# Moving a streaming kernel's SBUF arena from 32 bytes past a 256-byte boundary onto the boundary

## The chip, the cores and the metric

The kernel runs on one core of a Trainium2 chip. Times are device microseconds from repeated executions. A time that I call "the span" is that of the one execution that was profiled.

## The reference, cut to what matters

The input is 384 x 384 pixels of 384 channels in bf16, 113.25 MB. The kernel takes the mean of every channel, multiplies it by one weight, passes it through a sigmoid, and multiplies every pixel by the result:

```python
g = jnp.einsum("bhwc->bc", x) / (H * W)
s = sigmoid(g * w1d[0])          # k is 1, so the padding does nothing
return x * s[:, None, None, :]
```

Each byte has to be read and each has to be written: 226.5 MB in all.

## The kernel before: the parts that matter

SBUF holds one big tensor, the arena, which is cut into six slots of 44 rows. A chunk of 128 x 44 pixels is loaded into a slot, summed by matmuls with ones, multiplied in place by an early estimate of the gate, and stored. (The gate of the whole image is compared at the end; if it differs in bf16, a second pass repairs the output. It is not needed with these inputs.) So every pixel is read once and written once.

```python
total = nc.alloc_sbuf_tensor("total", [P, C], F32)
n_arena = nc.sbuf_bytes_remaining // (2 * C)
arena = nc.alloc_sbuf_tensor("arena", [P, n_arena * C], BF16)
...
EDGE, SLOT, BOTH = 44, 44, 4
def dram(view, r0, n):       # partition p gets n rows that lie together in memory
    return view[r0 * P : (r0 + n) * P, :].rearrange("(p t) c -> p (t c)", p=P)
def at(r0, n):
    return arena[:, r0 * C : (r0 + n) * C]
...
for k in range(BOTH):        # the first four chunks: half on each queue
    load(places[k], sizes[k], starts[k], ("sync", "scalar"))
...
for k in range(1, len(sizes)):
    if k >= n_slots:
        j = k - n_slots
        put(places[j], sizes[j], starts[j], places[j])    # gate on DVE, then store on the scalar queue
    if k >= BOTH:
        load(places[k], sizes[k], starts[k])              # on the sync queue, waits for that store
    add_rows(places[k], sizes[k], 1, k == 1, k == last)   # matmuls
```

In a partition the small tensors end at byte 20,000 = 78 x 256 + 32, and the arena starts there. One DMA moves 33,792 bytes (132 x 256) in each of 128 partitions, and one such piece is one data packet in the trace. The four opening chunks go in pieces of 16,896 bytes; the last two chunks have pieces of 21,504 and 18,432 bytes. All of these are multiples of 256.

Of the kernel before, what the change touches and what calls it, by code (L numbers as in the profile page):

```python
# [3 lines left out]
P = 128  # L4
ROW = 384
BF16 = mybir.dt.bfloat16
# [108 lines left out]
def bass_standalone__channel_attn_eca__vision_kernel(  # L115
# [5 lines left out]
    B, H, W, C = x.shape  # L121
# [13 lines left out]
    wrong = nc.alloc_sbuf_tensor("wrong", [P, 1], F32)  # L135
    redo = nc.alloc_sbuf_tensor("redo", [P, 1], I32)
    total = nc.alloc_sbuf_tensor("total", [P, C], F32)
    n_arena = nc.sbuf_bytes_remaining // (2 * C)
    arena = nc.alloc_sbuf_tensor("arena", [P, n_arena * C], BF16)
    acc = [  # L140
        [nc.alloc_psum_tensor(f"acc{g}_{i}", [P, WIDE], F32) for i in range(3)]
        for g in range(2)
# [258 lines left out]
```

## Time and profile before

| | before |
|---|---|
| time, median of 3 runs | 531.62 us (531.5 to 532.85) |
| packets of the two data queues, share of 16 engines | 53.4% + 46.0% |
| PE / DVE busy | 47% / 46% |
| rate, 85 to 185 us | 432 GB/s |
| data packet of 33,792 bytes, load or store | 1251 ns in 5,671 of 5,888 |

From the page of the kernel before: the span and the engines' busy times, then the span in 40 slices of 13 us (busy tenths of the DMA engines, and what they moved), then the two data queues (packets, MB, share of the 16 engines' span; q10 is fed by ScalarE's sequencer, q1 by SyncE's).

```profile
span 529.9 us, 1954 instructions
PE 246.9 (47%) x865; PEld 96.4 (18%) x865; DVE 241.2 (46%) x45; ACT 2.7 (1%) x4; POOL 0.3 (0%) x5
...
DMA  8999999999999999999999999999999999999997
GB/s 357 430 427 412 446 429 431 446 412 444 434 426 446 413 443 444 416 444 431 429 445 416 441 439 421 446 414 441 444 416 446 427 431 444 424 429 431 444 416 331
...
q10 hardware_dynamic: 4466, 121.90, 53.4%
q1 hardware_dynamic: 3888, 104.60, 46.0%
```

The DMA engines are full in all slices but the first and the last, while PE and DVE sit idle half of the time. The list of waits of the load queue says the same from the other side; its columns are what waited, for what, how long in total, how often, and the longest.

```profile
SPq L99 <- DMA out_dram<-arena: 454.2, 21, 63.1
```

Loads wait for stores to leave their slot. The kernel is bound by the DMA engines, which spend 53.4% + 46.0% = 99.4% of the span in packets of the two data queues. So I took it that anything that shortens a packet in the steady state shortens the kernel.

### The profile page before, as it was taken

To read this page: it belongs to the slowest core of one execution; us is meant where nothing else is said; L and a number is where in the kernel's file an instruction comes from. 1 tells how busy PE (TensorE), PEld (TensorE's weight loads), DVE (VectorE), ACT (ScalarE), POOL (GpSimd) and SP (SyncE) were. 2 spreads that over 40 slices of the span, in tenths; PEclk is the share of its full clock that TensorE was granted. 3 is DMA by queue.
4 is the path that set the end of the run, shared out by engine and by line. 5 is a ranking of instruction groups with operands and counts; after the bars stand their busy time and mean duration, and the time that the engine had idled before them with its cause. 6 is when DMAs were issued, how large, how long until landed. Compare 5 with 4: busy or idle time off the path is not lost.

```text
span 529.9 us, 1954 instructions
## 1 busy us (share of the span) xinstructions
PE 246.9 (47%) x865; PEld 96.4 (18%) x865; DVE 241.2 (46%) x45; ACT 2.7 (1%) x4; POOL 0.3 (0%) x5
## 2 busy tenths in 40 slices
PE   0977174264274274364264274373263373374400
PEld 0333021121021121121021121121121121121100
DVE  0199824633624624623624615615614615617620
ACT  1000000000000000000000000000000000000000
POOL 0000000000000000000000000000000000000000
PEclk9988675786786875786786875776886876777665
DMA  8999999999999999999999999999999999999997
GB/s 357 430 427 412 446 429 431 446 412 444 434 426 446 413 443 444 416 444 431 429 445 416 441 439 421 446 414 441 444 416 446 427 431 444 424 429 431 444 416 331
DMA packets 8363, 226.62 MB, mean 428 GB/s; under 512 B 930, under 2 KB 930, under 8 KB 930
## 3 DMA queue, kind: packets, MB, share of 16 engines
q10 hardware_dynamic: 4466, 121.90, 53.4%
q1 hardware_dynamic: 3888, 104.60, 46.0%
q8 instruction: 6, 0.10, 0.1%
q14 instruction: 3, 0.02, 0.0%
HBM read 113.25 MB, written 113.25 MB: 427 GB/s over the span
## 4 chain that ended last, share of the span: by engine, by line
another core or an unknown queue 70%; DMA 16%; DVE 4%; PE 3%; issue 1%; SPq 1%; ACT 0%; ACTq 0%
DMA out_dram<-arena 8%; DMA arena<-in_x_dram 6%; PE acc L186 3%; DMA w_one<-in_w1d_dram 2%; DVE arena L156 2%; SPq L91 1%; DVE total L208 1%; ACT s_true L290 0%; ACT s_early L266 0%; DVE total L298 0%; DVE total L206 0%; DVE wrong L306 0%; ACTq L91 0%; SPq L99 0%
## 5 line engine op out<-in xcount | busy, mean ns | idle before, releaser
L186 PE MATMUL acc<-arena,ones 128*128 128x512 bf16 x864 | 246.8, 457 | 242.3 <-DMA arena<-in_x_dram 242.3
L156 DVE TENSOR_TENSOR arena<-arena,s_early 128x16896 bf16<-128x16896 bf16 (+2 forms) x27 | 234.5, 8691 | 240.3 <-PE acc L186 236.1
L186 PEld LDWEIGHTS acc<-arena,ones 128*128 128x128 bf16 x864 | 96.3, 114 | 392.3 <-DMA arena<-in_x_dram 254.5
L234 PE MATMUL w_all<-w_one,ones 1*128 1x1 bf16 x1 | 0.2, 158 | 14.4 <-DMA w_one<-in_w1d_dram 14.4
L243 DVE TENSOR_SCALAR w_scaled<-w_all 128x1 f32<-128x1 f32 x2 | 0.2, 153 | 13.6 <-PE w_all L234 13.6
L208 DVE TENSOR_TENSOR total<-total,acc 128x128 f32<-128x128 f32 (+2 forms) x11 | 4.5, 408 | 1.7 <-PE acc L186 1.4
L206 DVE COPY total<-acc 128x384 f32<-128x384 f32 x1 | 0.6, 556 | 10.0 <-PE acc L186 10.0
L290 ACT ACTIVATE s_true<-total,w_scaled 128x384 bf16<-128x384 f32 x1 | 0.6, 614 | 478.2 <-DVE total L208 478.2
L234 PEld LDWEIGHTS w_all<-w_one,ones 1*128 1x128 bf16 x1 | 0.1, 98 | 14.4 <-issue 14.4
L228 ACT ACT_TABLE_LOAD x1 | 1.3, 1283 | 3.4 <-issue 3.4
L298 DVE TENSOR_TENSOR total<-s_true,s_early 128x384 f32<-128x384 uint16 x1 | 0.6, 557 | 0.7 <-ACT s_true L290 0.7
L266 ACT ACTIVATE s_early<-total,w_scaled 128x384 bf16<-128x384 f32 x1 | 0.6, 614 | 22.7 <-DVE total L208 22.7
L306 DVE TENSOR_REDUCE wrong<-total 128x1 f32<-128x384 f32 x1 | 0.6, 553 | 0.0
L256 DVE MEMSET ones<- 128x128 bf16 x1 | 0.2, 165 | 0.8 <-PEq L386 0.8
L228 ACT ACTIVATE warm<-warm 128x1 f32<-128x1 f32 x1 | 0.2, 203 | 0.0
L312 DVE CAST redo<-wrong 128x1 int32<-128x1 f32 x1 | 0.2, 153 | 0.0
L386 POOL MEMSET const-bfloat16-1.0<- 128x1 bf16 x1 | 0.1, 102 | 0.0
L386 POOL MEMSET const-uint8-127<- 128x1 uint8 x1 | 0.1, 102 | 0.0
L386 POOL MEMSET const-float32-0.0<- 128x1 f32 x1 | 0.1, 99 | 0.2 <-issue 0.2
L386 POOL MEMSET const-float32-1.0<- 128x1 f32 x1 | 0.1, 99 | 0.0
L255 POOL MEMSET warm<- 128x1 f32 x1 | 0.1, 98 | 0.3 <-POOLq L386 0.3
## 6 DMA issues: line engine op xcount, KB each, us to landing
out_dram<-arena ACTq DMA_DIRECT2D x25, 4224.0 KB, 61.5
arena<-in_x_dram SPq DMA_DIRECT2D x21, 4224.0 KB, 39.2
arena<-in_x_dram ACTq DMA_DIRECT2D x4, 2112.0 KB, 27.5
arena<-in_x_dram SPq DMA_DIRECT2D x4, 2112.0 KB, 27.5
arena<-in_x_dram SPq DMA_DIRECT2D x1, 2688.0 KB, 35.6
out_dram<-arena ACTq DMA_DIRECT2D x1, 2688.0 KB, 30.0
arena<-in_x_dram SPq DMA_DIRECT2D x1, 2304.0 KB
out_dram<-arena ACTq DMA_DIRECT2D x1, 2304.0 KB, 27.1
```

The costliest lines, as they stand in the source:

```text
L91: ("op", lambda e: e.dma_start(out, in_), self.pool[i], 16)
L156: return lambda e: e.tensor_tensor(to_v, v, s_b, ALU.mult)
L186: lambda e, i=i, bank=bank: e.matmul(bank[:, :], ones[:], arena[:, start + i * WIDE : start + (i + 1) * WIDE], start=first and i < 3, stop ...
L206: emit = lambda e, part=part, of=of: e.tensor_copy(part, of)
L208: emit = lambda e, part=part, of=of: e.tensor_tensor(part, part, of, ALU.add)
L228: lambda e: e.activation(warm[:, 1:2], warm[:, 0:1], ACT_F.Sigmoid),
L234: lambda e: e.matmul(w_all[:, 0:1], ones[0:1, :], w_one[0:1, 0:1], start=True, stop=True),
L266: lambda e: e.activation(s_early[:], total[:], ACT_F.Sigmoid, scale=w_scaled[:, 0:1]),
L290: lambda e: e.activation(s_true[:], total[:], ACT_F.Sigmoid, scale=w_scaled[:, 1:2]),
L298: lambda e: e.tensor_tensor(total[:], s_true[:].bitcast(U16), s_early[:].bitcast(U16), ALU.not_equal),
L306: lambda e: e.reduce_max(wrong[:], total[:], axis=mybir.AxisListType.X),
L386: nc = _bacc.Bacc("TRN2", target_bir_lowering=False, num_devices=1)
```

## The change

The change puts the arena at byte 20,224 = 79 x 256. As every piece is a multiple of 256 bytes long, every transfer then has its SBUF address at a multiple of 256, where it was 32 bytes past one. (Below, "misaligned" means off a multiple of 256.) There is still room for 272 rows, so there are six slots as before, and each engine has the same instructions in the same order.

```diff
-    n_arena = nc.sbuf_bytes_remaining // (2 * C)
-    arena = nc.alloc_sbuf_tensor("arena", [P, n_arena * C], BF16)
+    n_arena = (nc.sbuf_bytes_remaining - 256) // (2 * C)
+    arena = nc.alloc_sbuf_tensor("arena", [P, n_arena * C], BF16, align_bytes=256)
```

## The prediction

> **What bounds the kernel now.** The DMA engines. The page's slices show a mean DMA busy share of 90% or more in 38 of 40 slices; PE is busy 47% of the span, DVE 46%. The queue list puts 53.4% + 46.0% = 99.4% of the 16 engines' span into packets of the two data queues. In steady state (the stretch view, 85 to 185 us) the DMA share is 1.00 at 432 to 433 GB/s; only the start (401 GB/s) and the last 8 us (352 GB/s) are lower. So the time is the sum of packet durations per DMA engine plus about 3 us.
>
> **What a packet costs.** From the trace's packet records: a row piece of 33,792 bytes takes 1251 ns in loads and stores alike (5,671 of 5,888 exactly), 21,504 bytes take 799 and 18,432 take 686. The slope is 15,360 bytes in 565 ns = 27.2 bytes per ns[...]. The intercept is 1251 - 33,792/27.2 = about 8.6 ns per packet. A 4-byte semaphore packet, which does not touch the arena, takes 9 ns, so nearly all of those 8.6 ns look like a fixed cost.
>
> **What the change does.** The arena has room for 272 rows before; 256 bytes less still leaves 272, and six slots of 44 rows. Schedule, sizes, queues and waits stay; nothing is added or removed. Every row address moves from 32 bytes past a multiple of 256 to a multiple of 256. Row pieces are multiples of 256 bytes (33,792 = 132 x 256), so today every data packet is misaligned on the SBUF side, and afterwards none is; the HBM side steps in the same multiples already. I expect the gate (8691 ns) and the matmul (457 ns) unchanged.
>
> **What it should save.** [...] An engine moves 226.5 MB / 16 / 33,792 = 419 such packets[...]; the whole intercept would be 3.6 us (0.7%). All of it lies on the critical path, because the engines are saturated. [...]
>
> **Predicted time.** 531.0 us, 0.6 below the 531.62; range 529.4 to 532.5. Faster by over 2%: 0.01; within 2%: 0.97; slower by over 2%: 0.02.
>
> **What would show it.** The 33,792-byte packet drops from 1251 to 1247-1250 ns, most likely 1250; if it does not move, misalignment costs nothing at this size. DMA share stays 99%, steady rate 433 to 434 GB/s. The numbers of packets and instructions and the load queue's wait for stores (21 waits, 454 us) stay.
>
> **What would make it wrong.** [...] If aligned rows of all partitions collide in SBUF, with each other or with DVE and PE reads, packets would grow: slower. If alignment changes the DVE's or PE's rate, it would hardly show: half their time is idle.

The forecast's sum came to a gain of 0.6 us (531.62 - 531.0), which is 1.4 ns for each of the 419 packets of an engine. Terms of that sum are cut at the marks: the saving per packet that was held most likely, and a larger one, rested on a mechanism that no run of this case shows. Of the terms only the largest still stands, the whole intercept of 8.6 ns for each packet, 3.6 us. The reason given for 2% being out of reach is cut too, because it took 27.2 bytes per ns for a limit, and the packet records show it only as the slope between two sizes.

## The result, and the profile after

| | before | after |
|---|---|---|
| median of 5 runs | 531.68 us | 531.89 us |
| range | 531.5 to 532.85 | 531.64 to 532.48 |
| ratio, 95% interval | | 1.0003 (0.9991 to 1.0015) |
| data packet of 33,792 bytes | 1251 ns in 5,671 of 5,888 | 1251 ns in 5,653 of 5,888 |
| data packet of 16,896 bytes, between 4 and 41 us | 629 ns in 447 of 935; 487 slower, mean 634.6 ns | 629 ns in 933 of 941 |

In the counts of 16,896-byte packets, here and below, the one or two of each run that took over 645 ns (653 and 1127 ns in the kernel before) are left out.

The same lines of the page after:

```profile
span 530.1 us, 1954 instructions
PE 246.3 (46%) x865; PEld 96.0 (18%) x865; DVE 241.2 (45%) x45; ACT 2.7 (1%) x4; POOL 0.3 (0%) x5
...
DMA  8999999999999999999999999999999999999997
GB/s 357 432 431 408 439 418 449 426 430 441 418 446 428 428 447 421 436 439 421 444 425 433 444 421 439 436 419 449 426 431 441 419 444 431 428 428 438 438 420 334
...
q10 hardware_dynamic: 4466, 121.90, 53.5%
q1 hardware_dynamic: 3888, 104.60, 46.0%
```

and of its load queue's waits:

```profile
SPq L99 <- DMA out_dram<-arena: 454.1, 21, 63.1
```

Nothing that bounds the kernel moved: the queues' shares, the rate and the wait are those of before. (Single slices swing between 408 and 449. My estimate from the packet size: one packet of 33,792 bytes more or less on each of 16 engines in a slice of 13.25 us is 41 GB/s. The stretch from 85 to 185 us has 432 GB/s before and 433 after, and the packet records of 100 to 450 us give 432.9 for both.) One thing did move, in the packet records: in the opening, while only loads run, half of the 16,896-byte packets of the kernel before take about 5 ns more than 629 ns, and none but a few do after. The excess adds up to 0.17 us per DMA engine, too little to see in the time.

So there are two questions. Is misalignment really free for these packets, or is it paid somewhere that does not show? And is the slow opening due to alignment, or chance?

### The profile page after: what moved, and what is told of

The parts are those of the page before. It is cut to its first block, busy times and chain, and to the rows that moved or that the text cites. A ratio compares the mean times of both kernels' runs of the same rounds, so it can differ in the third digit from the quotient of the medians.

```text
span 530.1 us, 1954 instructions
## 1 busy us (share of the span) xinstructions
PE 246.3 (46%) x865; PEld 96.0 (18%) x865; DVE 241.2 (45%) x45; ACT 2.7 (1%) x4; POOL 0.3 (0%) x5
## 4 chain that ended last, share of the span: by engine, by line
another core or an unknown queue 70%; DMA 16%; DVE 4%; PE 3%; SPq 1%; issue 1%; ACT 0%; ACTq 0%
DMA out_dram<-arena 8%; DMA arena<-in_x_dram 6%; PE acc L186 3%; DVE arena L156 3%; DMA w_one<-in_w1d_dram 2%; SPq L91 1%; DVE total L208 1%; ACT s_true L290 0%; ACT s_early L266 0%; DVE total L298 0%; DVE total L206 0%; DVE wrong L306 0%; ACTq L91 0%; SPq L99 0%
## 5 line engine op out<-in xcount | busy, mean ns | idle before, releaser
L156 DVE TENSOR_TENSOR arena<-arena,s_early 128x16896 bf16<-128x16896 bf16 (+2 forms) x27 | 234.5, 8691 | 241.2 <-PE acc L186 237.8
```

Source lines behind the costliest of these rows:

```text
L156: return lambda e: e.tensor_tensor(to_v, v, s_b, ALU.mult)
```

## The experiments

In all but the two repeats the arena is allocated at a multiple of 256 bytes with 192 bytes of room, and shifted by a constant. All outputs were correct.

### Other offsets, and the two kernels once more

```diff
-    arena = nc.alloc_sbuf_tensor("arena", [P, n_arena * C], BF16, align_bytes=256)
+    SH = 2      # e_off4: 2 elements, 4 bytes; e_off128: SH = 64
+    arena = nc.alloc_sbuf_tensor("arena", [P, n_arena * C + 96], BF16, align_bytes=256)
...
-        return arena[:, r0 * C : (r0 + n) * C]
+        return arena[:, SH + r0 * C : SH + (r0 + n) * C]
...
-        start = place * C
+        start = SH + place * C
```

In the expectations below, a descriptor is the transfer of one contiguous run, which is one packet in these traces (e_768_off0 has 295,851 packets; 226.5 MB in runs of 768 bytes are 294,912). The theories were there to be tested. A: the start address costs nothing. B: an offset of 4 bytes costs something, 32 and 128 bytes do not. C: a small cost per transfer, larger at 128 bytes past than at 32. D: a larger cost per transfer than C. The mechanisms that the theories were drawn from are cut at the marks, because no run of this case shows them; the bands that are left are my guesses.

Expected of e_off4:

> The aligned kernel with the arena shifted to 4 bytes past a multiple of 256[...]. Theory A (start address free[...]): the 33,792-byte packet stays 1251 ns, time within 0.3% of before. Theory B[...]: packet 1252 to 1260 ns, time 0.1 to 0.8% up (532 to 536 us).

Expected of e_off128:

> Arena at 128 bytes past a multiple of 256. Theories A and B: packet 1251 ns, time within 0.3% of before. Theory C[...] packet 1256 ns and time about 2 us up against the aligned kernel.

Expected of the kernel before, run again unchanged:

> The kernel before once more, for its packet records. In its first trace the 16,896-byte load packets between 22 and 42 us took 633 or 640 ns (466 of them), in the trace after all 629. If alignment does that (a cost in the load-only opening), they show 633 and 640 here again. If it was chance of that one execution, they may all show 629.

Expected of the changed kernel, run again unchanged:

> The changed kernel once more. If alignment decides the 629 against 633 or 640 ns of the load-only opening: all 629 again. If chance decides: 633 and 640 may turn up here too. 33,792-byte packets 1251 ns.

| arena, bytes past a multiple of 256 | time (ratio to before, interval) | 33,792-byte packets at 1251 ns | 16,896-byte packets from 4 to 41 us: slower than 629 ns, their mean | excess per engine | first slow ones at about |
|---|---|---|---|---|---|
| 0 (e_after_again) | one run | 5,666 of 5,888 | 4 of 941 | 0.00 us | none |
| 4 (e_off4) | 531.84 us (1.0003, 0.9989 to 1.0017) | 5,479 | 582 of 936, 635.6 ns | 0.24 us | 18 us |
| 32 (e_before_again) | one run | 5,650 | 490 of 940, 634.6 ns | 0.17 us | 21 us |
| 128 (e_off128) | 531.96 us (1.0003, 0.9989 to 1.0016) | 5,655 | 286 of 940, 634.1 ns | 0.09 us | 26 us |

The time and the whole-row packet do not depend on the offset, from 0 to 128 bytes (531.68 to 531.96 us in the four kernels timed; at 4 bytes 137 whole-row packets read 1252 ns and 25 read 1249, but the mean of all is 1252.9 ns, against 1253.0 to 1253.4 in the other five traces). The DVE gate takes 8691 ns when aligned and 8693 ns at 4 bytes past. The slow opening is alignment and not chance: both traces of the misaligned kernel have it, both of the aligned kernel lack it, and the other two offsets have it in their own size. It does not grow with the distance from the multiple of 256 below: 128 bytes past cost no more than 32. The excess is even smaller there: from 30 to 41 us, where the packets have turned slow, all of them together average 635.7, 634.6 and 632.8 ns at 4, 32 and 128 bytes, that is 6.7, 5.6 and 3.8 ns above 629 (at 128 bytes a quarter of them still take 629). Why the offset matters so is open. In the opening of every misaligned kernel here the packets, once the start is over, are at 629 ns for 15 to 24 us first; I come back to that.

### The same bytes in short runs

To make a cost per transfer visible, the next kernels move the same bytes in runs of 256 or 768 bytes (the matching reshapes of the SBUF side are left out of the diff).

```diff
 # e_768_*: row t*128+p in partition p, so that a run in memory is one row
-        return view[r0 * P : (r0 + n) * P, :].rearrange("(p t) c -> p (t c)", p=P)
+        return view[r0 * P : (r0 + n) * P, :].rearrange("(t p) c -> p t c", p=P)
 # e_256_*: three DMAs for each old one, one for each third of every row
+        v = view[r0 * P : (r0 + n) * P, :].rearrange("(p t) c -> p t c", p=P)
+        return [v[:, :, b * D : (b + 1) * D] for b in range(3)]      # D = C // 3
 # SH = 0 in e_*_off0, SH = 16 elements (32 bytes) in e_*_off32
```

Expected of e_256_off0:

> The same work moved in runs of 256 bytes (three DMAs for each old one, one per third of a row), arena at a multiple of 256. [...]if a fixed 8.6 ns comes on each as it does on a whole row, 9.4 + 8.6 = 18 ns instead of 9.4, and the time nearly doubles (about 1000 us); [...]it is between 535 and 900 us. This is the base for e_256_off32, whichever it is.

(The band of 535 to 900 us was for a fixed part that not every run pays.)

Expected of e_256_off32:

> As e_256_off0 with the arena 32 bytes past a multiple of 256: every run of 256 bytes now crosses a boundary[...]. Theory A (alignment to 256 is free): same time as e_256_off0 within 1%. Theory C[...] 6 to 12% slower than e_256_off0. Theory D[...]: over 12% slower.

Expected of e_768_off0:

> The same work moved in runs of 768 bytes (row t*128+p in partition p), arena at a multiple of 256. [...]540 to 700 us. Base for e_768_off32.

(The band came from 768 / 27.2 = 28.2 ns for the bytes of a run, and up to 8.6 ns more.)

Expected of e_768_off32:

> As e_768_off0 with the arena 32 bytes past a multiple of 256[...]. Theory A: same as e_768_off0 within 1%. Theory C: [...]3 to 4% slower. Theory D: over 4% slower.

| run | aligned | 32 bytes past | difference of the medians |
|---|---|---|---|
| 256 bytes | 792.01 us (1.4899 of before) | 836.17 us (1.5723) | 44.2 us, 5.6% |
| 768 bytes | 614.36 us (1.1562) | 625.69 us (1.1764) | 11.3 us, 1.8% |

So misalignment is not free. But neither difference is one that I had written down: 5.6% is just below the band of theory C (6 to 12%), and 1.8% lies between theory A (within 1%) and theory C (3 to 4%). The slices say why. First e_768_off0, then e_768_off32, the rate in 40 slices of the span:

```profile
GB/s 306 373 372 373 373 373 373 373 372 373 373 373 373 373 372 373 373 373 373 373 372 373 373 373 373 373 372 373 373 373 373 372 373 373 373 373 372 373 373 332
```

```profile
GB/s 277 326 326 341 373 373 373 373 372 373 373 373 373 373 372 373 373 373 373 373 372 373 373 373 373 373 372 373 373 373 372 372 373 373 373 373 372 359 324 293
```

The loss is all in the first four slices and the last three. In between, the misaligned kernel runs at exactly the rate of the aligned one. Stretches of e_768_off32 give the three parts; the columns are the stretch, its length, busy time of PE, PEld, DVE, ACT and POOL with the number of instructions, the granted TensorE clock, the DMA share and GB/s:

```profile
6.00:56.00 50.00, 29.91 (x100) 11.49 (x100) 20.89 (x11) 2.10 (x3) 0.00 (x0) 0.86 1.10 326
60.00:570.00 510.00, 212.58 (x746) 82.80 (x744) 206.51 (x24) 0.00 (x0) 0.00 (x0) 0.70 1.09 373
590.00:615.00 25.00, 0.00 (x0) 0.00 (x0) 1.26 (x3) 0.61 (x1) 0.00 (x0) 0.50 1.02 322
```

In the packet records the slow part starts at about 4.5 us and ends at 57 us, and the first store packet starts at 57.1 us. The last load packet starts at 570.3 us, and the end turns slow at about 585 us. So the cost is paid where the engines move in one direction only, and not where loads and stores alternate. The two slow parts account for the difference: 52 us x (1 - 326/373) = 6.6 us, and 37 us x (1 - 322/373) = 5.1 us, together 11.6 us before rounding, for 11.3 us measured.

The runs of 256 bytes show the same, but for small losses in the middle. The slices of e_256_off0, then of e_256_off32:

```profile
GB/s 254 289 289 278 290 290 290 290 290 290 290 290 290 289 290 290 290 290 290 289 290 290 290 290 289 290 290 290 290 290 289 290 290 290 290 289 285 289 290 238
```

```profile
GB/s 198 218 218 218 256 288 289 289 289 280 286 290 290 290 282 285 289 290 289 290 282 286 286 289 286 281 287 290 290 289 283 286 290 289 289 287 234 216 216 184
```

Three stretches of e_256_off32, loads alone, both, stores alone:

```profile
6.00:60.00 54.00, 18.77 (x67) 7.41 (x67) 2.75 (x8) 0.00 (x0) 0.00 (x0) 0.91 1.39 218
200.00:300.00 100.00, 36.06 (x127) 14.12 (x128) 26.87 (x3) 0.00 (x0) 0.00 (x0) 0.65 1.28 289
760.00:820.00 60.00, 0.00 (x0) 0.00 (x0) 0.00 (x0) 0.00 (x0) 0.00 (x0) 0.51 0.85 216
```

and those of e_256_off0:

```profile
6.00:60.00 54.00, 28.08 (x100) 11.00 (x100) 3.80 (x9) 2.10 (x3) 0.00 (x0) 0.91 1.28 289
200.00:300.00 100.00, 31.72 (x109) 12.22 (x110) 26.87 (x3) 0.00 (x0) 0.00 (x0) 0.64 1.28 290
740.00:780.00 40.00, 0.00 (x0) 0.00 (x0) 0.00 (x0) 0.00 (x0) 0.00 (x0) 0.50 1.28 290
```

In the middle, from 100 to 740 us, e_256_off32 averages 287.1 GB/s by its packet records, for 289.5 in the middle of e_256_off0, which is about 5 of the 44 us. In two of its dips, at 180 to 190 and 300 to 310 us, the load queue has 54% and 55% of the packets instead of half: there the mixture is uneven.

From the rates, the cost of one misaligned run follows (16 engines, so one engine's time per run is 16 x bytes / rate):

| run | aligned, ns per run | loads alone, 32 bytes past | extra | stores alone, extra |
|---|---|---|---|---|
| 256 bytes | 16 x 256 / 290 = 14.1 | 16 x 256 / 218 = 18.8 | 4.7 ns | 16 x 256 / 216 - 14.1 = 4.8 ns |
| 768 bytes | 16 x 768 / 373 = 32.94 | 16 x 768 / 326 = 37.69 | 4.7 ns | 16 x 768 / 322 - 32.94 = 5.2 ns |

The extra is the same for both sizes, so it is a cost per run and not per byte. (The durations of single packets are no good for this: a 256-byte packet is recorded as 18 ns while one ends every 14.1 ns. The records overlap: 18 / 14.1 = 1.28, the DMA share that the stretches of e_256_off0 show.)

### Loads and stores kept apart

That the mixture of directions hides the cost was still only read off from where the slow parts lay. A rival says that it belongs to the opening and the end of the program for some other reason, for example because the opening loads on both queues. The last four kernels load six chunks, then store all six, then load the next six, on one queue for each direction after the opening. The rival then expects nothing new in the later batches.

```diff
-    for k in range(1, len(sizes)):
-        ... (a store of chunk k-6, then the load of chunk k)
+    for b in range(0, len(sizes), n_slots):
+        ks = range(b, min(b + n_slots, len(sizes)))
+        if b:
+            for token in stored_of[-1]:      # loads wait for all stores of the last batch
+                plan._wait("sync", token)
+        ... load and add all ks (new lists of tokens)
+        for token in landed[-1]:             # stores wait for all loads of this batch
+            plan._wait("scalar", token)
+        for k in ks:
+            put(places[k], sizes[k], starts[k], places[k])
```

Expected of e_768_split_off0:

> 768-byte runs, aligned arena, but loads and stores kept apart: six chunks are loaded, then all six are stored, then the next six are loaded, in five batches. Both theories: 768-byte packets 36 ns throughout, 373 GB/s within a load or store phase, 640 to 720 us in all because of the gaps between phases. Base for e_768_split_off32.

Expected of e_768_split_off32:

> The same 32 bytes off. In e_768_off32 only the opening (326 for 373 GB/s, 4.7 ns per descriptor) and the end were slower than in e_768_off0; the stretch in which loads and stores alternate was not. Theory M (a misaligned SBUF side costs about 4.7 ns per descriptor, and shows only where an engine moves in one direction): every phase is slow, 18,432 descriptors per engine times 4.7 ns = 87 us above e_768_split_off0 (60 to 95). Theory E (it belongs to the opening and the end of a program, whatever the direction): 11 us above, as between e_768_off32 and e_768_off0.

Expected of e_row_split_off0:

> Whole rows of 33,792 bytes, aligned, loads and stores kept apart in five batches: 560 to 620 us. Packets 1251 ns in all phases. Base for e_row_split_off32.

Expected of e_row_split_off32:

> The same 32 bytes off. Theory M: in later load phases too the packets turn from 1251 to about 1255 to 1262 ns, after some 30 packets per engine if the slack of about 150 ns seen in the opening is used up again in each phase; time 0.5 to 2 us above e_row_split_off0. Theory E: 1251 ns in all phases after the opening, same time.

| loads and stores apart | aligned | 32 bytes past | difference of the medians |
|---|---|---|---|
| 768-byte runs | 642.77 us (1.2079 of before) | 728.40 us (1.3699) | 85.6 us, 13.3% |
| whole rows, 33,792 bytes | 558.59 us (1.0501) | 561.15 us (1.0550) | 2.6 us, 0.46% |

The rival expected 11 us for the first pair, the theory of the direction 87 us. 85.6 us were measured; over the 18,432 runs that each engine moves that is 4.6 ns for one. The rates in 40 slices, first of e_768_split_off0, then of e_768_split_off32:

```profile
GB/s 310 373 372 373 307 373 373 373 373 313 372 373 373 303 373 373 373 373 314 373 372 373 306 373 373 373 373 314 372 373 372 306 373 373 373 373 311 327 248 343
```

```profile
GB/s 281 326 327 326 272 325 323 325 325 287 326 326 326 268 324 323 325 325 287 326 326 326 270 324 323 324 325 285 326 326 327 272 325 325 323 325 286 326 243 305
```

The dips in both are the changes of direction. Between them every phase, loads and stores, is at 373 GB/s when aligned and at 323 to 327 when not. Nothing else differs between the two kernels, and the mixed kernels of the same run length do not show it in their middle. This settles the direction against the rival. Nor is it two queues taking turns that hides the cost: in the opening of e_768_off32, from 10 to 46 us, each queue has half of the packets (7,651 and 7,647), all of them loads, and the rate is 326 GB/s.

With whole rows the effect is as small as it should be: an engine moves 419 of them, and 419 x 4.7 ns = 2.0 us; 2.6 us were measured, and the intervals of the two ratios to before (1.0483 to 1.0518 and 1.0532 to 1.0567) do not meet. (Two expectations were narrowly missed here: 2.6 us is above the 0.5 to 2 us, and the aligned kernel's 558.59 us is below 560.) Each of the four full store phases, 48 packets per engine, is 0.23 to 0.26 us longer than in the aligned kernel, 5 ns for a packet. Its packet records show it directly:

| packets of 33,792 bytes | aligned | 32 bytes past |
|---|---|---|
| second load phase, 150 to 165 us | all 192 at 1251 ns | 173 of 192 at 1251 ns |
| second load phase, 165 to 185 us | 255 of 256 at 1251 ns | 3 of 254 at 1251 ns, mean 1255.4 ns |
| first store phase, 85 to 120 us | all 448 at 1251 ns | 48 of 448 at 1251 ns, mean 1255.9 ns |

A load phase again starts at 1251 ns and turns slow some 35 us later, so the delay of the opening repeats in the second, third and fourth load phase; the fifth, 23 us long, does not turn slow. An estimate from the opening of the whole-row kernels, packets per engine before the slow ones times the excess of 30 to 41 us: 31 x 5.6 ns at 32 bytes, 25 x 6.7 ns at 4 bytes and 39 x 3.8 ns at 128 bytes, 147 to 174 ns. So some 150 ns of cost (an estimate from these counts) do not show when the loads start; why, no run shows. The short runs do not fit one number as well (some 60 runs of 768 bytes, 2 us, before the first slow ones), and stores do not agree among themselves: in the split whole-row kernel they are slow within 12 us of the first one, in e_768_off32 the stores of the end only 15 us after the last load, and in the kernel before not at all in the 30 us after its last load (1251, 799 and 686 ns, as after the change). So the delay is not explained.

## Why the prediction was right or wrong

- **The bound: right.** The DMA engines bound both kernels, with 99.4% and 99.5% of their span in data packets.
- **No instruction, size or wait changes: right.** The wait of the load queue is 454.2 and 454.1 us, the gate 8691 ns on average in both, the matmul 457 and 456 ns.
- **The time: within the range, but the small gain that the point stood for did not come.** The range, 529.4 to 532.5 us, held the unchanged time as well, so the hit says nothing for the mechanism; as far as that goes it was luck. Predicted 531.0 us, 0.6 us below the time then; measured 531.89 us, 0.2 us above before, with an interval of -0.09% to +0.15%. A gain of 0.6 us (0.11%) lies just outside of it.
- **The packet drops to 1247 to 1250 ns, most likely 1250: wrong.** It stayed at 1251 ns. The prediction went on that misalignment then "costs nothing at this size". That was wrong as well: with loads and stores apart the same packet takes 1255 to 1256 ns.
- **The step that failed: "All of it lies on the critical path, because the engines are saturated."** The engines are saturated, but a misaligned SBUF address is not paid by the engine that alternates between loads and stores (373 GB/s in the middle of the 768-byte kernel, aligned or not). Only the opening paid, 0.17 us per engine, and the time does not show that much.
- **The size was off too.** I took about 1 ns per packet (1251 to 1250) as the most likely cost. At 32 bytes past the boundary the runs show 4.6 to 5.6 ns for one transfer, from 256 bytes to whole rows (the 5.6 is the opening of the kernel before), and no more at 128 bytes past it (3.8 ns in the opening). It is a cost per misaligned transfer, nearer to half of the 8.6 ns intercept than to 1 ns. The two errors had opposite signs.
- **The 8.6 ns intercept overstates the cost of a packet.** The records overlap: at 432.9 GB/s (100 to 450 us) a whole row leaves an engine every 1249.0 ns, 2 ns less than its record, so 6.6 ns are left above its bytes at the slope of 27.2 bytes per ns. From rates, an aligned run of 256 bytes takes 14.1 ns and its bytes 256 / 27.2 = 9.4 ns, so the fixed part is 4.7 ns; at 768 bytes it is 32.9 - 28.2 = 4.7 ns again.
- **No sign of collisions of aligned rows in SBUF: as hoped.** The 33,792-byte packet is at 1251 ns before and after, with a mean of 1253.0 and 1253.2 ns.

What is shown and what is not: it is shown that the cost exists, that it belongs to a transfer and not to a byte moved (4.7 ns for 256 and for 768 bytes), that it is paid by loads alone and by stores alone (326 and 322 GB/s for 373, with 768-byte runs), and that alternating the two hides it (373 GB/s in the middle of both 768-byte kernels), all but some 5 us of it with 256-byte runs. Why alternating hides it is not shown: no run looks inside the engine.

## What to carry to other kernels

Ask of a cost per transfer how many transfers there are and whether the side that pays is the one that sets the pace: 4.7 ns on 1251 ns is 0.4% even where it is paid, and here it was not. Align SBUF buffers to 256 bytes when runs are short and a phase moves in one direction, where it was worth 12.6% of the rate at 768 bytes (326 for 373 GB/s, loads alone) and 25% at 256 (218 for 290); where whole rows of 33,792 bytes alternated between loads and stores, it was worth nothing measurable (ratio 1.0003, interval 0.9991 to 1.0015). And when a difference falls between two theories, look at where in the span it lies before you fit a number to the mean.
